# AdaLN attention and gated MLP in one kernel: output sums carried in PSUM, gates that read one factor from PSUM

## The chip, the cores and the metric

The kernel runs on one core of a Trainium2 chip. The metric is the time of one execution in device microseconds. The program is traced in the order in which it is written: each engine (PE for matmuls, DVE for vector operations, ACT for activations and copies, POOL, SP for DMA issues) works through its own queue in that order, and semaphores hold an instruction until its inputs are there and its output's old readers are done.

## The reference

One transformer block over 2048 tokens of width 576. Six modulation rows come from a small vector `c`. The first half is attention of 32 query heads of 128 over the last 512 keys of 16 cached key and value heads; the second half is an MLP of inner width 4608, gated by a rectifier.

```python
mod = (_silu(c) @ w_mod).reshape(c.shape[0], 6, 1, -1)      # sa, ca, ga, sb, cb, gb
h = _layernorm(x) * (1 + ca) + sa
x = x + ga * attention(h)         # softmax(q k^T / sqrt(128)) v, then @ wo, K and V: last 512 rows
h = _layernorm(x) * (1 + cb) + sb
gate, up = h @ W_gate, h @ W_up
x = x + gb * ((gate * (gate > 0) * up) @ W_down)
```

## The kernel before

Every large matmul is done in a split form: an operand is cut into a rounded part (`hi`) and the rest (`lo`), and three products make one. ACT makes `hi` by a copy, POOL makes `lo` by a subtraction.

**State.** `acc[0..15]` are sixteen tiles of 128 tokens x 576 in SBUF. They hold x, collect the attention's output and then the MLP's, and are stored at the end.

**Attention.** There are NU = 128 units: 16 key heads, 4 blocks of 512 tokens, 2 query heads each. The main loop (L1176 to L1225) writes out the order of one unit u by hand, with places `run(u, 0)` to `run(u, 9)` at which a table of further steps (weight loads and cuts, layer norms, modulation sums) is worked in. For unit u, PE does the scores (`s_half`, L407 to L409), the projection of the next unit's queries (`qproj`, L360), one small matmul `qm` (`spread`, L433), a first output piece, the two halves of the product with v for unit u-1 (`pv_half`, L507 to L509), and a second output piece.

DVE takes the scores' block maxima (L412), reduces them to 16 a partition (`max_pre`, L419), multiplies them by a mask of four columns (L420) and reduces the last unit's sums of exponentials (`sum_pre`, L426). `qm` spreads the masked maxima and the sums over the partitions; the tile of `qm` is a PSUM bank of the pool `psM`, which has two, shared with the projection and the product with v. Then DVE finds the maximum (L448) and the sum's inverse (L438), subtracts the maximum (L480), and ACT takes the exponential (L482) and makes its `hi` (L469). POOL sums the exponentials (L495, L498) and makes `lo` (L489).

**Output pieces.** `wo_piece` multiplies the outputs of two heads by their rows of wo for one tile of 128 tokens: 12 matmuls of 288 columns (L536) into the two banks of `psW`. That pool has one buffer, which some layer norm transposes and modulation rows use too. `down_piece` returns a function that adds the banks to `acc` on DVE (L542); the loop puts it in `pend` and calls it by `flush()` a few steps later. A piece can start only when the piece before it has been read out.

**MLP.** 36 rounds m, each with seven products P1 to P7 (a scheme in which seven products of sums of blocks do the work of eight), in the order P1, P6, P2, P7, P5, P4, P3. A product makes gate and up for 512 tokens in the two halves of a PSUM pair (`prod`, L834). P2 goes on in P1's pair and P3 in P5's. `evac` reads the pair out: running sums `q` and `r` are kept in SBUF, and four of the products end in a gate, max(gate, 0) times up, whose result `h_out` cuts into `hhi` on ACT (L849) and `hlo` on POOL (L850). Between the halves of a product stand the output pieces of the round before (`md_piece`, the same L536 and L542, `psW`). In the first 18 rounds the weights are also combined (`w_prep`: L647, L651, L652, L657 on DVE), cut (L627 on ACT, L628 and L629 on POOL) and stored for the second 18, and the rows of W_down are gated (L216) and cut (L175, L176). In rounds 2 to 15 layer norms (`ln_half`) and sums for the later tokens (`h_later`, L752, L764, L767) are worked in.

Of the kernel before, what the change touches and what calls it, by code (L numbers as in the profile page):

```python
# [32 lines left out]
def kernel(  # L33
# [119 lines left out]
    def gate_row(j):  # L153
        r = cp.tile([P, D], F32, tag="mrow", name=f"mrow{j}")
        mod_row(j, r, 0.0)
        return r
# [88 lines left out]
        else:  # L245
            nc.sync.dma_start(dst[:96], hb[qb, 4][j].rearrange("r p n -> (r p) n"))

    pend = []
    ready = {}
    adds = [0] * (S // P)  # L250

    def flush():
        while pend:
            pend.pop()()

    class LayerNorm:
        def __init__(self, qb, key, where):
# [157 lines left out]

    def max_pre(u):
        t5[u] = sp.tile([P, 5, 16], F32, tag="t5", name=f"t5_{u}", bufs=1)
        t = t5[u][:, 4, :]
        nc.vector.tensor_reduce(t, t4.pop(u).rearrange("p k b -> p b k"), axis=AX.X, op=ALU.max)  # L419
        nc.vector.tensor_tensor(t5[u][:, 0:4, :], mask[:, :, None].to_broadcast([P, 4, 16]),  # L420
                                t[:, None, :].to_broadcast([P, 4, 16]), op=ALU.mult)
# [7 lines left out]

    def spread(u):  # L430
        a, b = (0 if u < NU else 4), (5 if u else 4)
        bps[u] = psM.tile([P, 512], F32, tag="mm", name=f"qm{u}")
        nc.tensor.matmul(bps[u][:, a * 16:b * 16], quad,  # L433
                         t5.pop(u)[:, a:b, :].rearrange("p a b -> p (a b)"), start=True, stop=True)

# [89 lines left out]
    def down_piece(his, los, ws, i, qt, nm, mid=None, pool=None):  # L525
        sl = slice(qt * P, (qt + 1) * P)
        pool = pool or (psW, "w")
        ps = pool[0].tile([P, 2, 512], F32, tag=pool[1], name=nm)
        for half in range(2):
            if half and mid:  # L530
                mid()
            cs = slice(half * H2, (half + 1) * H2)
            n = 0
            for hi, lo, w in zip(his, los, ws):
                for a, b in ((hi, 0), (hi, 1), (lo, 0)):
                    nc.tensor.matmul(ps[:, half, :H2], a[:, sl], w[:, b, cs],  # L536
                                     start=(n == 0), stop=(n == 5))
                    n += 1
        av = acc[i].rearrange("p (h n) -> p h n", h=2)

        def add():
            nc.vector.tensor_tensor(av, ps[:, :, :H2], av, op=ALU.add)  # L542
            adds[i] += 1

        return add

    def wo_piece(u1, qt, mid=None):
        g, qb, h = unit(u1)
        return down_piece([ohi[u1 - 1], ohi[u1]], [olo[u1 - 1], olo[u1]], [wos[h - 1], wos[h]],
                          4 * qb + qt, qt, f"wo{u1}_{qt}", mid)  # L550

# [287 lines left out]
    def h_out(m, f, k, r):  # L839
        pool, tag = HI[f, k]  # L840
        hi = hhi[m, f, k] = pool.tile([P, 512], F32R, tag=tag, name=f"hhi{m}_{f}{k}")
        if k == 0:
            pool, tag, w = op, "olo", 512
        elif f == 1:
            pool, tag, w = qp, ("qlo", "qhi")[m % 2], 512
        else:
            pool, tag, w = xp, "xm", 640
        lo = hlo[m, f, k] = pool.tile([P, w], F32R, tag=tag, name=f"hlo{m}_{f}{k}")[:, :512]
        nc.scalar.copy(hi, r)  # L849
        nc.gpsimd.tensor_sub(lo, r, hi.bitcast(F32))  # L850

    def gated(m, f, k, c):
        nc.vector.scalar_tensor_tensor(c[:, 0, :], c[:, 0, :], 0.0, c[:, 1, :], op0=ALU.max, op1=ALU.mult)
        h_out(m, f, k, c[:, 0, :])

    npair, px = [0], {}

# [8 lines left out]
    def evac(m, s):  # L866
        ps = pair[m, s]
        if s == "P1":
            t = tmp["q"] = pp.tile([P, 2, 512], F32, tag="hi", name=f"q{m}")
            nc.scalar.copy(t, ps)  # L870
        elif s == "P2":
            r = xp.tile([P, 640], F32, tag="xm", name=f"r{m}")[:, :512]
            nc.scalar.activation(r, ps[:, 0, :], AF.Relu, bias=0.0, scale=1.0)
            nc.vector.tensor_tensor(r, ps[:, 1, :], r, op=ALU.mult)
            h_out(m, 0, 0, r)
        elif s == "P6":
            nc.vector.tensor_tensor(tmp["q"], ps, tmp["q"], op=ALU.add)
        elif s == "P7":
            t = tmp["r"] = pp.tile([P, 2, 512], F32, tag="lo", name=f"r{m}", bufs=2)
            nc.vector.tensor_tensor(t, ps, tmp["q"], op=ALU.add)  # L880
        elif s == "P5":
            t = pp.tile([P, 2, 512], F32, tag="lo", name=f"c22_{m}", bufs=2)
            nc.vector.tensor_tensor(t, ps, tmp["r"], op=ALU.add)
            gated(m, 1, 1, t)
        elif s == "P4":
            nc.vector.tensor_tensor(tmp["r"], ps, tmp["r"], op=ALU.add)
            gated(m, 1, 0, tmp["r"])
        else:
            nc.vector.tensor_tensor(tmp["q"], ps, tmp["q"], op=ALU.add)
            gated(m, 0, 1, tmp["q"])  # L890

    def wd_prep(m, f):
        tag = "wB" if f else "wC"
# [37 lines left out]
    def step(name, t, fn, *args):  # L931
        sched.append((t + PLAN.get(name, 0), len(sched), fn, args))
# [14 lines left out]
    def setd(d, k, fn):  # L947
        def go():
            d[k] = fn()
        return go  # L950
# [6 lines left out]
    def norm_steps(nm, qb, key, w2, w3, t_st, t_rs, t_nm, t_tr, t_af, how):  # L957
        ln = LayerNorm(qb, key, xms[:2] + where[w2] + where[w3])
        how = CFG.get(nm, how)
        for i in range(4):  # L960
            step(f"{nm}.st{i}", t_st[i], ln.stats, i)
        step(f"{nm}.rs", t_rs, ln.rstd)
        for i in range(4):
            step(f"{nm}.nm{i}", t_nm[i], ln.norm, i)
        for k, ds in enumerate(((0, 1), (2, 3), (4,))):
            pool = pools[how[k][0]]
            tag = {"s": "s", "w": "w", "m": "mm"}[how[k][0]]
            step(f"{nm}.tr{k}", t_tr[k], ln.trans, ds, pool, tag)
            step(f"{nm}.af{k}", t_af[k], ln.affine, ds, *((pp, "p") if qb < 2 and key == "a" else (bp, "bc")),
                 how[k][1:])  # L970

# [38 lines left out]
    step("v0.c", 1, pv0[1])  # L1010
    for t in range(5):
        step(f"m2.{t}", (4, 4, 14, 14, 16)[t], lambda t=t: mod_step(2, t, big[2, t]))
    step("ga", 19, setd(mods, "ga", lambda: gate_row(2)))
    norm_steps("a2", 2, "a", "wC", "raw", (8, 9, 14, 14), 16, (19,) * 4, (29, 26, 29),
               (29, 26, 29), (("w", "aav", "vvv"), ("w", "vvv", "vvv"), ("m", "aav")))
# [159 lines left out]
    run(-1, 9)  # L1175
    for u in range(NU):  # L1176
        u0, q0 = (u - 4, 3) if u % 2 else (u - 3, 1)
        u1, q1 = (u - 2, 0) if u % 2 else (u - 3, 2)
        run(u, 0)
# [12 lines left out]
        spread(u)  # L1192
        max_bc(u)
        if u + 1 < NU:
            q_hi(u + 1)
        run(u, 3)
        if 0 < u0 < NU - 8:
            pend.append(wo_piece(u0, q0))
        run(u, 4)
        if u:  # L1200
            pv_half(u - 1, 0)
        exp_half(u, 0)
        ksum_op(u, 0)
# [11 lines left out]
        if 0 < u1 and (q1 == 0 or u1 < NU - 8):  # L1215
            pend.append(wo_piece(u1, q1))
# [65 lines left out]
```

## Time and profile before

| | |
|---|---|
| median of 3 runs | 3110.5 us (3109.76 to 3110.93) |
| the profiled execution | 3113.83 us |
| its span, first to last instruction | 3112.0 us |
| mean granted PE clock | 0.977 |
| attention, about | 0 to 1700 us |
| MLP, about | 1700 to 3112 us |

The page has one profiled execution; its numbers are compared with that execution's own time. A group's line names the kernel line, the engine, the operation, the tiles and shapes, the count, then the busy time, the mean of one, and the idle time of the engine before the group. A line of the list of waits names who waited for whom, the total in us, the count and the longest. A line of the timeline gives the start and duration in us, and in brackets how long the engine stood before it and for whom.

### The profile page before, as it was taken

The numbers are of one execution on the slowest core, as the hardware profiler recorded it, in microseconds if no ns is written. First come the engines' busy times: TensorE is split into PE (matmuls) and PEld (weight loads), VectorE is DVE, ScalarE is ACT, GpSimd is POOL, SyncE is SP. The second block draws the span as 40 slices with busy tenths as digits, with TensorE's granted clock in tenths as the row PEclk, the third lists the DMA queues.
The fourth block names the chain that finished last, engine by engine and source line by source line (L and its number), as shares of the span: only waits on it lengthen the run. The fifth ranks groups of instructions, "written<-read, shape, count | busy, mean of one in ns | idle before, by whom it ended". The sixth has DMA issues, their size and how long they took to land. (4 is left out here: it accounts for less than half of the span.)

```text
span 3112.0 us, 40062 instructions
## 1 busy us (share of the span) xinstructions
PE 2945.5 (95%) x15414; PEld 2533.0 (81%) x15414; DVE 2225.0 (71%) x2904; ACT 1082.2 (35%) x1399; POOL 1981.7 (64%) x1386
## 2 busy tenths in 40 slices
PE   6899999999999999999987699999999999999999
PEld 5688888888888888888876588887787888888888
DVE  7888888888898888888875666666766544444444
ACT  5444444444444444444443233333222211111110
POOL 5788999888888898888975555556656311111111
PEclk9999999999999999999998799999999999999999
DMA  4101111211111100000002356557777954444443
GB/s 144 38 24 54 62 65 62 68 54 55 46 45 48 34 25 26 16 16 20 24 30 95 119 201 213 210 209 260 255 256 248 329 175 173 157 162 162 170 169 114
DMA packets 143647, 360.24 MB, mean 116 GB/s; under 512 B 12768, under 2 KB 52448, under 8 KB 143456
## 3 DMA queue, kind: packets, MB, share of 16 engines
q1 hardware_dynamic: 115312, 245.15, 24.6%
q10 hardware_dynamic: 28144, 112.54, 9.2%
q8 instruction: 121, 1.98, 0.3%
q14 instruction: 70, 0.57, 0.1%
HBM read 234.62 MB, written 151.32 MB: 124 GB/s over the span
## 5 line engine op out<-in xcount | busy, mean ns | idle before, releaser
L489 POOL TENSOR_TENSOR lo<-p,hi 128x1024 fp32r<-128x1024 f32 x256 | 607.7, 2395 | 0.0
L536 PE MATMUL md<-wogb,hhi 128*128 128x288 f32 x2304 | 482.8, 302 | 50.8 <-DVE acc L542 31.3
L834 PE MATMUL gu<-hop_T,wop 128*128 128x512 f32 (+1 forms) x2016 | 505.6, 396 | 16.5 <-ACT hop_T L684 11.7
L542 DVE TENSOR_TENSOR acc<-md,acc 128x576 f32<-128x576 f32 x288 | 217.3, 755 | 413.0 <-PE md L536 412.8
L536 PEld LDWEIGHTS md<-wogb,hhi 128*128 128x128 f32 x2304 | 391.9, 193 | 86.8 <-DVE acc L542 44.7
L834 PEld LDWEIGHTS gu<-hop_T,wop 128*128 128x128 f32 (+1 forms) x2016 | 372.4, 190 | 88.3 <-ACT hop_T L684 12.2
L536 PE MATMUL wo<-woga,ohi 128*128 128x288 f32 x2048 | 427.3, 301 | 11.0 <-DVE acc L542 9.7
L360 PE MATMUL qps<-hTa,wA 128*128 128x512 f32 x1792 | 430.5, 391 | 1.9 <-DVE hTa L344 1.1
L498 POOL TENSOR_TENSOR ks<-ks,p 128x512 f32<-128x512 f32 x256 | 345.8, 1351 | 95.1 <-ACT p L482 81.7
L360 PEld LDWEIGHTS qps<-hTa,wA 128*128 128x128 f32 x1792 | 338.4, 189 | 73.8 <-POOL hTa L348 1.8
L834 PE MATMUL gu<-hop_B,wop 128*128 128x512 f32 (+1 forms) x1512 | 388.4, 400 | 6.8 <-DVE hop_B L688 3.6
L412 DVE TRANSPOSE_TENSOR_REDUCE t<-s 128x32 f32<-128x1024 f32 x256 | 318.8, 1247 | 77.2 <-PE s L409 64.5
L536 PEld LDWEIGHTS wo<-woga,ohi 128*128 128x128 f32 x2048 | 334.0, 189 | 25.7 <-DVE acc L542 14.5
L850 POOL TENSOR_TENSOR hlo<-r,hhi 128x512 fp32r<-128x512 f32 x72 | 93.8, 1303 | 401.2 <-ACT hhi L849 334.8
L536 PE MATMUL md<-wogb,hlo 128*128 128x288 f32 x1152 | 346.0, 300 | 1.0 <-POOL hlo L850 1.0
L834 PEld LDWEIGHTS gu<-hop_B,wop 128*128 128x128 f32 (+1 forms) x1512 | 286.0, 194 | 65.6 <-DVE hop_B L688 4.0
L482 ACT ACTIVATE p<-p 128x1024 f32<-128x1024 f32 x242 | 256.0, 1058 | 137.8 <-DVE p L480 108.6
L536 PE MATMUL wo<-woga,olo 128*128 128x288 f32 x1024 | 303.0, 296 | 0.0
L480 DVE TENSOR_TENSOR p<-s,mb 128x1024 f32<-128x1024 f32 x242 | 294.9, 1219 | 3.8
L469 ACT CAST hi<-p 128x1024 fp32r<-128x1024 f32 x256 | 269.6, 1053 | 7.9
L536 PEld LDWEIGHTS md<-wogb,hlo 128*128 128x128 f32 x1152 | 222.0, 193 | 1.2 <-POOL hlo L850 1.2
L542 DVE TENSOR_TENSOR acc<-wo,acc 128x576 f32<-128x576 f32 x256 | 192.4, 751 | 39.9 <-PE wo L536 26.4
(176 smaller groups left out, 5043.5 us busy)
## 6 DMA issues: line engine op xcount, KB each, us to landing
wk_P<-wop ACTq DMA_DIRECT2D x126, 640.0 KB
wop<-wk_P SPq DMA_DIRECT2D x126, 640.0 KB
wr<-wlay SPq DMA_DIRECT2D x72, 384.0 KB
dk<-wogb ACTq DMA_DIRECT2D x36, 576.0 KB
wogb<-dk SPq DMA_DIRECT2D x36, 576.0 KB
rogb<-wd SPq DMA_DIRECT2D x36, 288.0 KB
rwA<-wq SPq DMA_DIRECT2D x32, 320.0 KB
wlay<-wg SPq DMA_DIRECT2D x36, 256.0 KB
```

Of the source, the lines that this page charges most:

```text
L360: return [lambda i=i, a=a, b=b: nc.tensor.matmul(ps, a, b, start=(i == 0), stop=(i == n - 1)) for i, (a, b) in enumerate(ops)]
L412: nc.vector.tensor_reduce(t4[u][:, 2 * h:2 * h + 2, :].rearrange("p k b -> p (k b)"), t.rearrange("p k (b j) -> p (k b) j", j=32), axis=AX ...
L469: nc.scalar.copy(hi_[u, h], pt[u, h])
L480: nc.vector.tensor_tensor(p, t, bc[u][:, None, :].to_broadcast([P, 2, 512]), op=ALU.subtract)
L482: nc.scalar.activation(p, p, AF.Exp, bias=0.0, scale=1.0)
L489: nc.gpsimd.tensor_sub(lo_[u, h], pt[u, h], hi_[u, h].bitcast(F32))
L498: nc.gpsimd.tensor_tensor(ks_[u], ks_[u], p[:, j, :], op=ALU.add)
L536: nc.tensor.matmul(ps[:, half, :H2], a[:, sl], w[:, b, cs], start=(n == 0), stop=(n == 5))
L542: nc.vector.tensor_tensor(av, ps[:, :, :H2], av, op=ALU.add)
L834: nc.tensor.matmul(ps, a, c, start=s not in ("P2", "P3") and i == 0, stop=i == len(ops) - 1, skip_group_check=True)
L850: nc.gpsimd.tensor_sub(lo, r, hi.bitcast(F32))
```

## The change

Three edits.

First, output pieces that follow another piece in `psW` with no other user between (`seeded`) no longer start their own sums. ACT copies the `acc` tile of the next piece into the banks (`put_seed`), the piece's matmuls add to it, and ACT copies the banks back to `acc`. The function that does both is put in a list of its own, `pend_act`, which is worked off ahead of `exp_half(u, 0)` for the first piece of a unit and behind `hi_half(u, 1)` for the second. Pieces that follow another user of `psW` are done as before.

Second, the gates. `gated` reads gate and up from the PSUM pair: it adds the running sum to the gate half into SBUF, adds it to the up half in place in PSUM, and takes max(gate, 0) times up with up in PSUM. P2's rectifier goes from ACT to DVE. Since P3 goes on in P5's pair, whose up half now holds a sum, P7's up half is copied by ACT into `q` and subtracted.

Third, `max_pre` writes the reduced maxima into columns 128 to 143 of the bank of `qm`, and the mask multiplies them from there; so the bank is taken in `max_pre` and not in `spread`.

```diff
+    def flush(q=None):
+        q = pend if q is None else q
+        while q:
+            q.pop()()
...
     def max_pre(u):
         t5[u] = sp.tile([P, 5, 16], F32, tag="t5", name=f"t5_{u}", bufs=1)
-        t = t5[u][:, 4, :]
+        bps[u] = psM.tile([P, 512], F32, tag="mm", name=f"qm{u}")
+        t = bps[u][:, 128:144]
         nc.vector.tensor_reduce(t, t4.pop(u).rearrange("p k b -> p b k"), axis=AX.X, op=ALU.max)
...
     def spread(u):
         a, b = (0 if u < NU else 4), (5 if u else 4)
-        bps[u] = psM.tile([P, 512], F32, tag="mm", name=f"qm{u}")
+        if u == NU:
+            bps[u] = psM.tile([P, 512], F32, tag="mm", name=f"qm{u}")
...
                     nc.tensor.matmul(ps[:, half, :H2], a[:, sl], w[:, b, cs],
-                                     start=(n == 0), stop=(n == 5))
+                                     start=(n == 0 and seed is None), stop=(n == 5),
+                                     skip_group_check=seed is not None)
...
         def add():
+            adds[i] += 1
+            if seed is not None:
+                nc.scalar.copy(av, ps[:, :, :H2])
+                return
             nc.vector.tensor_tensor(av, ps[:, :, :H2], av, op=ALU.add)
-            adds[i] += 1
...
+    w_use, pieces, seeds = set(), [], {}
+
+    def seeded(n):
+        return 0 < n < len(pieces) and not any(pieces[n - 1][0] < t <= pieces[n][0] for t in w_use)
+
+    def put_seed(n):
+        if seeded(n):
+            u1, qt = pieces[n][1:]
+            g, qb, h = unit(u1)
+            s = seeds[n] = psW.tile([P, 2, 512], F32, tag="w", name=f"wo{u1}_{qt}")
+            nc.scalar.copy(s[:, :, :H2], acc[4 * qb + qt].rearrange("p (h n) -> p h n", h=2))
+
+    def piece(n):
+        add = wo_piece(*pieces[n][1:], seed=seeds.get(n))
+
+        def end():
+            add()
+            put_seed(n + 1)
+
+        (pend_act if n in seeds else pend).append(end)
+        return n in seeds
...
-    def gated(m, f, k, c):
-        nc.vector.scalar_tensor_tensor(c[:, 0, :], c[:, 0, :], 0.0, c[:, 1, :], op0=ALU.max, op1=ALU.mult)
-        h_out(m, f, k, c[:, 0, :])
+    def gated(m, f, k, ps, r, a, op1=ALU.add):
+
+        if a is None:
+            nc.vector.tensor_scalar(r, ps[:, 0, :], 0.0, None, op0=ALU.max)
+        else:
+            nc.vector.tensor_tensor(r, ps[:, 0, :], a[:, 0, :], op=ALU.add)
+            nc.vector.tensor_tensor(ps[:, 1, :], ps[:, 1, :], a[:, 1, :], op=op1)
+        nc.vector.scalar_tensor_tensor(r, r, 0.0, ps[:, 1, :], op0=ALU.max, op1=ALU.mult)
+        h_out(m, f, k, r)
...
         elif s == "P2":
-            r = xp.tile([P, 640], F32, tag="xm", name=f"r{m}")[:, :512]
-            nc.scalar.activation(r, ps[:, 0, :], AF.Relu, bias=0.0, scale=1.0)
-            nc.vector.tensor_tensor(r, ps[:, 1, :], r, op=ALU.mult)
-            h_out(m, 0, 0, r)
+            gated(m, 0, 0, ps, xp.tile([P, 640], F32, tag="xm", name=f"r{m}")[:, :512], None)
...
         elif s == "P7":
             t = tmp["r"] = pp.tile([P, 2, 512], F32, tag="lo", name=f"r{m}", bufs=2)
             nc.vector.tensor_tensor(t, ps, tmp["q"], op=ALU.add)
+            nc.scalar.copy(tmp["q"][:, 1, :], ps[:, 1, :])
         elif s == "P5":
             t = pp.tile([P, 2, 512], F32, tag="lo", name=f"c22_{m}", bufs=2)
-            nc.vector.tensor_tensor(t, ps, tmp["r"], op=ALU.add)
-            gated(m, 1, 1, t)
+            gated(m, 1, 1, ps, t[:, 0, :], tmp["r"])
         elif s == "P4":
-            nc.vector.tensor_tensor(tmp["r"], ps, tmp["r"], op=ALU.add)
-            gated(m, 1, 0, tmp["r"])
+            gated(m, 1, 0, ps, tmp["r"][:, 0, :], tmp["r"])
         else:
-            nc.vector.tensor_tensor(tmp["q"], ps, tmp["q"], op=ALU.add)
-            gated(m, 0, 1, tmp["q"])
+
+            gated(m, 0, 1, ps, tmp["q"][:, 0, :], tmp["q"], ALU.subtract)
...
         run(u, 3)
-        if 0 < u0 < NU - 8:
-            pend.append(wo_piece(u0, q0))
+        if 10 * u + 3 in at:
+            piece(at[10 * u + 3])
         run(u, 4)
         if u:
             pv_half(u - 1, 0)
+        flush(pend_act)
         exp_half(u, 0)
...
         run(u, 8)
         hi_half(u, 1)
+        flush(pend_act)
         lo_half(u, 0)
```

More of the change, by code (lines that the diff above doesn't have):

```diff
@@ L246, in hb_load @@
             nc.sync.dma_start(dst[:96], hb[qb, 4][j].rearrange("r p n -> (r p) n"))
-    pend = []
+    pend, pend_act = [], []
     ready = {}
     adds = [0] * (S // P)
-    def flush():
-        while pend:
-            pend.pop()()
+    def flush(q=None):
+        q = pend if q is None else q
+        while q:
+            q.pop()()
     class LayerNorm:
@@ L523, in o_lo, with down_piece @@
         nc.gpsimd.tensor_sub(olo[u], o.pop(u), ohi[u].bitcast(F32))
-    def down_piece(his, los, ws, i, qt, nm, mid=None, pool=None):
+    def down_piece(his, los, ws, i, qt, nm, pool=None, seed=None):
         sl = slice(qt * P, (qt + 1) * P)
         pool = pool or (psW, "w")
-        ps = pool[0].tile([P, 2, 512], F32, tag=pool[1], name=nm)
+        ps = pool[0].tile([P, 2, 512], F32, tag=pool[1], name=nm) if seed is None else seed
         for half in range(2):
-            if half and mid:
-                mid()
             cs = slice(half * H2, (half + 1) * H2)
@@ L541, in add, with wo_piece @@
         def add():
+            adds[i] += 1
+            if seed is not None:
+                nc.scalar.copy(av, ps[:, :, :H2])
+                return
             nc.vector.tensor_tensor(av, ps[:, :, :H2], av, op=ALU.add)
-            adds[i] += 1
         return add
-    def wo_piece(u1, qt, mid=None):
+    def wo_piece(u1, qt, seed=None):
         g, qb, h = unit(u1)
         return down_piece([ohi[u1 - 1], ohi[u1]], [olo[u1 - 1], olo[u1]], [wos[h - 1], wos[h]],
-                          4 * qb + qt, qt, f"wo{u1}_{qt}", mid)
+                          4 * qb + qt, qt, f"wo{u1}_{qt}", seed=seed)
+    w_use, pieces, seeds = set(), [], {}
[14 more added lines that the diff above has]
+        return n in seeds
     NFP = NFT // 2
@@ L968, in norm_steps @@
             step(f"{nm}.tr{k}", t_tr[k], ln.trans, ds, pool, tag)
+            if tag == "w":
+                w_use.add(t_tr[k])
             step(f"{nm}.af{k}", t_af[k], ln.affine, ds, *((pp, "p") if qb < 2 and key == "a" else (bp, "bc")),
@@ L1012 @@
         step(f"m2.{t}", (4, 4, 14, 14, 16)[t], lambda t=t: mod_step(2, t, big[2, t]))
+    w_use.update((19, e - 41, e - 21))
     step("ga", 19, setd(mods, "ga", lambda: gate_row(2)))
@@ L1173, in run @@
             fn(*args)
-    run(-1, 9)
     for u in range(NU):
@@ L1178 @@
         u1, q1 = (u - 2, 0) if u % 2 else (u - 3, 2)
+        if 0 < u0 < NU - 8:
+            pieces.append((10 * u + 3, u0, q0))
+        if 0 < u1 and (q1 == 0 or u1 < NU - 8):
+            pieces.append((10 * u + 6, u1, q1))
+    at = {t: n for n, (t, _, _) in enumerate(pieces)}
+    run(-1, 9)
+    for u in range(NU):
         run(u, 0)
@@ L1214 @@
             pv_half(u - 1, 1)
-        if 0 < u1 and (q1 == 0 or u1 < NU - 8):
-            pend.append(wo_piece(u1, q1))
+        if 10 * u + 6 in at:
+            piece(at[10 * u + 6])
         run(u, 7)
```

## The prediction

> **What bounds the kernel now.** I read the page's busy times first, then busy time by stretch, then the starts of one matmul that every attention unit has once, and only then the waits.
>
> ```profile
> span 3112.0 us, 40062 instructions
> PE 2945.5 (95%) x15414; PEld 2533.0 (81%) x15414; DVE 2225.0 (71%) x2904; ACT 1082.2 (35%) x1399; POOL 1981.7 (64%) x1386
> ...
> 160.00:1580.00 1420.00, 1407.68 (x7370) 1205.27 (x7369) 1254.12 (x1771) 650.21 (x774) 1265.01 (x775) 1.00 0.13 41
> 1580.00:1790.00 210.00, 150.47 (x670) 122.14 (x669) 133.39 (x172) 72.61 (x105) 112.91 (x87) 0.84 0.26 90
> 1790.00:2440.00 650.00, 604.41 (x3171) 522.22 (x3170) 420.53 (x416) 202.34 (x293) 390.81 (x358) 0.96 0.67 233
> 2440.00:3112.00 672.00, 664.71 (x3673) 588.46 (x3671) 285.82 (x326) 77.21 (x114) 103.83 (x82) 1.00 0.51 175
> ```
>
> The columns after each stretch are its length, then PE, PEld, DVE, ACT and POOL busy, then the granted clock. PE is the bound everywhere, and the change leaves the list of matmuls as it is. So the change can win only time in which PE stands: 12 us by this view in the attention, 60 in the passage to the MLP, 46 in the MLP's first half, 7 in the second half. But a busy PE hides short stalls, since a matmul's end is modelled. The unit's own beat shows them: the start of the `qm` matmul, one pair per unit.
>
> ```profile
> 143.60 0.45 PE L433 MATMUL qm<-t,quad 128*128 128x80 f32 x2
> ...
> 1001.90 0.45 PE L433 MATMUL qm<-t,quad 128*128 128x80 f32 x2
> ...
> 1014.28 0.45 PE L433 MATMUL qm<-t,quad 128*128 128x80 f32 x2
> ...
> 1063.18 0.34 PE L433 MATMUL qm<-t,quad 128*128 128x80 f32 x2
> ...
> 1076.76 0.45 PE L433 MATMUL qm<-t,quad 128*128 128x80 f32 x2 [0.54 <-DVE t L426]
> ...
> 1432.58 0.34 PE L433 MATMUL qm<-t,quad 128*128 128x80 f32 x2
> ...
> 1480.84 0.34 PE L433 MATMUL qm<-t,quad 128*128 128x80 f32 x2
> ...
> 1578.34 0.34 PE L433 MATMUL qm<-t,quad 128*128 128x80 f32 x2
> ```
>
> From 1432.58 to 1480.84 lie four units in which `qm` is not held: 12.06 us each. The unit 1001.90 to 1014.28 took 12.38, that from 1063.18 to 1076.76 took 13.58. From 143.60 to 1578.34 are 116 units; at 12.06 they would take 1399, and they took 1434.7. So 36 us are lost in the attention's steady part, three times what the busy column shows. What holds `qm`:
>
> ```profile
> PEld qm L433 <- DVE t L426: 45.7, 66, 3.8
> ...
> 1010.93 4.75 POOL L489 TENSOR_TENSOR lo<-p,hi 128x1024 fp32r<-128x1024 f32 x2
> ...
> 1012.67 0.74 DVE L420 TENSOR_TENSOR t<-mask,t 128x64 f32<-128x64 f32 x1
> 1013.51 0.71 DVE L426 TRANSPOSE_TENSOR_REDUCE t<-ks 128x16 f32<-128x512 f32 x1
> ...
> 722.91 1.41 POOL L176 TENSOR_TENSOR woga<-roga,woga 128x576 fp32r<-128x576 f32 x1
> ...
> 725.94 0.23 DVE L420 TENSOR_TENSOR t<-mask,t 128x64 f32<-128x64 f32 x1
> ...
> L420 DVE TENSOR_TENSOR t<-mask,t x128: 224/564/2169, 42.3 to 1686.3; 128x64 f32<-128x64 f32 x128
> ```
>
> L420 multiplies 64 elements a partition. With POOL idle (at 725.94, POOL's last row ended at 724.32) it takes 0.23; in the unit of 1014.28 it takes 0.74 and ends at 1013.41, just behind the first of POOL's two L489 (half of 4.75 after 1010.93 is 1013.3). It waits for POOL while both read SBUF. Behind it stands L426, and `qm` waits for L426.
>
> **The change part by part.** (1) L420 gets its maximum from PSUM, so one of its inputs leaves SBUF. Does that free it of POOL? The MLP's rows answer:
>
> ```profile
> L853 DVE SCALAR_TENSOR_TENSOR r<-r x36: 691/694/3518, 1761.9 to 3092.0; 128x512 f32<-128x512 f32 x36
> ...
> L880 DVE TENSOR_TENSOR r<-gu,q x36: 1206/1225/1226, 1749.1 to 3081.1; 128x1024 f32<-128x1024 f32 x36
> ```
>
> With both inputs in SBUF (L853) the longest is five times the median; with one in PSUM (L880) the longest equals the median. So I take 0.23 for L420 (bounds: 0.22, its minimum, and 0.56, its median now). L426 ends 0.5 us earlier; it was late by about 0.33 (12.38 less 12.06), so nearly all these waits go. 66 waits are listed in the whole run; some 60 lie in the steady part, at 0.36 (0.33, and more in a few long ones): -22. The wait that comes next is that for DVE's two L412 before it, which the 0.23 leaves 0.2 or more ahead of PE. The bank of `qm` is taken earlier, in front of the next projection; two banks are free then, nothing waits.
>
> (2) A piece's sum leaves DVE for two ScalarE copies: out to `acc`, then the next piece's seed.
>
> ```profile
> L542 DVE TENSOR_TENSOR acc<-wo,acc 128x576 f32<-128x576 f32 x256 | 192.4, 751 | 39.9 <-PE wo L536 26.4
> ...
> PE wo L536 <- DVE acc L542: 9.7, 13, 3.0
> ...
> 1003.48 0.63 ACT L519 CAST ohi<-rb 128x512 fp32r<-128x512 f32 x1 [7.01 <-PE wo L536]
> ...
> 1004.01 0.59 ACT L387 ACTIVATE qhi<-qps 128x512 fp32r<-128x512 f32 x1
> ...
> 1004.50 0.66 ACT L175 CAST woga<-roga 128x576 fp32r<-128x576 f32 x1
> ...
> 1006.56 0.42 PE L536 MATMUL wo<-woga,ohi 128*128 128x288 f32 x2
> ...
> L870 ACT COPY q<-gu 128x1024 f32<-128x1024 f32 x36 | 36.6, 1016 | 103.0 <-PE gu L834 47.7 <-POOL wop L629 38.9 <-PE pv L508 6.2
> ```
>
> DVE loses some 230 adds of 0.75, 1.5 us a unit, off the bound. ACT gains two copies a piece. No row shows ACT writing PSUM; the nearest are L175, 0.66 for 576 elements within SBUF, and L870, 1.02 for 1024 out of PSUM. I take 0.65, so 1.3 a pair (bounds 1.2 and 2.04). ACT goes from 650 of 1420 us to about 950: room enough. The point is place: the first pair stands ahead of the exponential of its unit, and piece two now waits for it. In the tight unit (every second one, where `ohi` waits for the first piece) `qhi` ends at 1004.60 and piece two starts at 1006.56: 1.96 for a pair of 1.3. Where the cast of `woga` stands there too (one unit in eight, the one shown), 1.96 for 1.96, and PE would wait 0.3 or so: 15 units, +4. The exponentials come 0.6 to 0.9 later; behind them wait POOL's L495, L498 and L489. POOL is busy 1265 of 1420, so it takes this up in its waits for `p`; `lo` is then ready about 1 us before PE reads it, where it was 2. I cost that at nothing; if POOL fell back one more cast (1.4 us) in one unit of eight, it would be +5. The waits for DVE's add in the attention's long units (13.58) and a shorter DVE queue before the column sums of the modulation give back the rest:
>
> ```profile
> 718.41 0.58 PE L164 MATMUL mps<-ones,macc 128*128 128x1 f32 x2 [2.00 <-DVE macc L161]
> ...
> 718.00:724.00 6.00, 5.59 (x14) 4.53 (x15) 1.77 (x3) 0.00 (x0) 6.00 (x4) 0.50 0.00 0
> ...
> 1589.94 2.17 DVE L420 TENSOR_TENSOR t<-mask,t 128x64 f32<-128x64 f32 x1
> ...
> 1593.08 0.42 PE L433 MATMUL qm<-t,quad 128*128 128x80 f32 x2 [1.58 <-DVE t L426]
> ```
>
> In front of L161 stood an add of 0.75, so of the 2.00 some 0.7 go, and with ten long units at 0.4 I take -4.5. The last units before the MLP hold the worst L420 (2.17); its wait of 1.58 goes, others there shrink by 0.5 each: -3. Units before 143 us: -1.
>
> The row of 718 to 724 has clock 0.50 after a wait of 2.00; if the shorter wait keeps the clock, up to 3 us more are won there, which I keep for the range. [...]
>
> (3) Gating. P5, P4 and P3 have now a 1024 add out of PSUM (1.23) and L853; after, two 512 adds and L853 with its second factor in PSUM. A 512 of L853 without POOL is 0.69, so three are 2.07 against 1.92: +0.15 each. P2 loses ACT's step and gains one of 0.69 on DVE, P7 gains a 0.6 copy on ACT. P3's matmuls go on in P5's bank and now wait for P5's L853, not its first add; between lies the whole product of P4. P7's copy waits for P7's add on DVE, and behind it in ACT's queue stand the next stores' issues and the cast of the weights for three products later, behind that cast POOL's L628 and L629: all with products to spare. In the MLP's second half DVE is busy 286 of 672: hidden behind the next product, 0; without that cover it would be 0.45 + 0.69 in each of 36 rounds, 41 us. In the first half DVE is late:
>
> ```profile
> PE md L536 <- DVE acc L542: 31.3, 20, 5.0
> DVE r L874 <- ACT r L873: 68.3, 36, 4.2
> ...
> 2250.50 3.52 DVE L853 SCALAR_TENSOR_TENSOR r<-r 128x512 f32<-128x512 f32 x1
> ...
> 2248.86 1.28 POOL L850 TENSOR_TENSOR hlo<-c,hhi 128x512 fp32r<-128x512 f32 x1 [2.29 <-ACT hhi L849]
> ...
> 2252.04 1.42 POOL L176 TENSOR_TENSOR wogb<-rogb,wogb 128x576 fp32r<-128x576 f32 x1
> 2254.75 1.26 POOL L850 TENSOR_TENSOR hlo<-r,hhi 128x512 fp32r<-128x512 f32 x1 [1.29 <-ACT hhi L849]
> ```
>
> PE waits 31 us for DVE's adds. Here L853 took 3.52, until POOL's run from 2248.86 to 2253.46 ended. Freed of that, it would take 0.69. But right behind it DVE has the weights' differences (L651, L652), both inputs in SBUF, and they would meet the same run of POOL: the wait moves on more than it goes. What stays won is one L853, 0.7, in each of 18 rounds, less 0.3 of longer adds: -7. Bounds: all of the 31 us, and some clock with them, -40; and +16 (below).
>
> [...]
>
> **Sum:** -22 + 4 - 4.5 - 3 - 1 + 0 - 7 = -33.5. The profiled execution took 3113.8 with its span of 3112.0, so 3080; the median of the runs, 3110.5, is 3.3 lower: 3077.
>
> **Rivals.** The first half clears too: L651 and L652 slip in before POOL's run, and the clock stays up; 25 us more, 3052. For it: L874's waits for ACT vanish from DVE's queue. Against: POOL's run is there whatever DVE does.
>
> The moved wait grows: a quicker gate makes `hhi` quicker, so POOL goes on into `hlo` of r (1.3, the row at 2254.75) before L651 gets its turn. 18 rounds at 1.3 in place of -0.4 are +23: the stage loses 16 and not wins 7, 3100. For it: POOL's gap of 1.29 at 2254.75 is there only because DVE was late.
>
> Seeds come late (slower): PE waits at piece two, in every second unit, from a pair longer than 1.96 on. It turns the sign where 58 such units lose 33.5 us, 0.58 each, a pair of 2.5; at 2.7 it is 43 us, 3120. Against: it is above the upper bound of 2.04.
>
> It doesn't do what it says: an input in PSUM does not spare L420. Then the 22 stay, and L853 stays as it is: about -4.5 -1 +4, 3109. Against: L880's flat durations.
>
> **How the numbers follow.** Forecast 0.64, clears too 0.13, moved wait 0.12, seeds late 0.06, no effect 0.05. The range takes in the first three, the -40 of the first half too (3044), and a pair at its bound of 2.04 (0.1 in 58 units, 0.7 in 15, less the 4: +12): 3044 to 3103. A measurement can tell about 0.2%, 6 us, from no change. Faster: 0.64 + 0.13 + most of 0.12 = 0.87; same: the rest of it and the 0.05, 0.07; slower: 0.06.
>
> **What would show it.** Right: L420 with a longest near its shortest, the list of waits without `qm` for L426, 12.1 us from `qm` to `qm`, L853 flat at 0.69, and longer L651 and L652. Wrong: PE waiting for ScalarE at `wo`, PE waiting for `lo` at L509, ACT copies of 576 above 0.98, or more waits at `md` than 31 us.

## The result, and the profile after

The changed kernel takes 3063.3 us (median of 4 runs, 3058.6 to 3067.9); the kernel before, run beside it on the same chip, 3110.7. The ratio is 0.9845, with a 95% interval of 0.9827 to 0.9863: 47 us faster, where 33.5 were forecast. The profiled execution took 3058.6, the shortest of the four, and the profiled one before 3113.8, so the two traces differ by 55 us and not by 47; the rest of this section explains the 55. Stage by stage it is read from these two traces, and the table below gives the other runs beside them.

The page of the changed kernel, span and busy times:

```profile
span 3056.8 us, 40707 instructions
PE 2914.2 (95%) x15414; PEld 2533.1 (83%) x15414; DVE 2027.2 (66%) x2810; ACT 1360.2 (44%) x1875; POOL 1988.1 (65%) x1386
```

The matmuls are the same 15414, and PE's busy time is nonetheless 31 us less. Since both kernels run the same matmuls in the same order, a stage's gain can be read as the difference between the starts of the same matmul. Busy time in the stretch from the first steady `qm` to the last, before and after (columns as in the prediction: length, PE, PEld, DVE, ACT, POOL, clock):

```profile
143.60:1578.34 1434.74, 1422.42 (x7445) 1218.03 (x7445) 1267.07 (x1787) 656.93 (x781) 1277.76 (x783) 1.00 0.13 41
```
```profile
144.20:1551.71 1407.51, 1406.00 (x7445) 1226.47 (x7444) 1075.37 (x1555) 931.20 (x1245) 1276.47 (x783) 1.00 0.13 42
```

The same 7445 matmuls take 27.2 us less: 12.13 a unit against 12.37. DVE gave up 192 us, ACT took on 274. And the stretch of the MLP's first half whose 3171 matmuls took 650.00 us before:

```profile
1761.09:2386.87 625.78, 591.18 (x3171) 514.93 (x3170) 400.85 (x481) 199.06 (x292) 397.82 (x358) 0.98 0.68 242
```

24.2 us less. Only 11.0 of that is time in which PE stood (650.00 less 604.41 is 45.6 before, 625.78 less 591.18 is 34.6 now). The other 13.2 is PE itself being quicker over the same matmuls, and the mean clock of the stretch rose from 0.96 to 0.98.

Single lines of the changed kernel (shortest, median and longest in ns, then first and last start). L422 is the old L420, L889 the old L853; L546 and L570 are the copy out and the seed:

```profile
L422 DVE TENSOR_TENSOR t<-mask,qm x128: 220/221/223, 41.7 to 1654.6; 128x64 f32<-128x64 f32 x128
...
L546 ACT COPY acc<-wo x238: 624/635/647, 111.0 to 1573.1; 128x576 f32<-128x576 f32 x119
...
L570 ACT COPY wo<-acc x238: 635/644/647, 107.1 to 1568.5; 128x576 f32<-128x576 f32 x119
...
L889 DVE SCALAR_TENSOR_TENSOR c<-c,gu x36: 686/686/689, 1724.4 to 3032.2; 128x512 f32<-128x512 f32 x36
```

L422's longest is 3 ns above its shortest; before, it reached 2169. L889 is as flat, where L853 reached 3518. Both now take one operand from PSUM.

A unit with a cast of `woga` in front of the pair, where a wait of PE was forecast:

```profile
985.79 0.59 ACT L388 ACTIVATE qhi<-qps 128x512 fp32r<-128x512 f32 x1
986.28 0.67 ACT L175 CAST woga<-roga 128x576 fp32r<-128x576 f32 x1
986.85 0.65 ACT L546 COPY acc<-wo 128x576 f32<-128x576 f32 x1
987.52 0.64 ACT L570 COPY wo<-acc 128x576 f32<-128x576 f32 x1
...
988.35 0.43 PE L537 MATMUL wo<-woga,ohi 128*128 128x288 f32 x2
```

The seed ends at 988.16 and piece two starts at 988.35, with no wait. In the stretch from 160 to 1580 the lists of waits of PE and of its weight loads have no `qm` in them; outside it, at the two ends of the attention, 5 waits of the weight load for the old L426 are left, 10.1 us of the 45.7. The head of PE's list, and the head of the same list from 1761 to 2387 (total us, count, longest):

```profile
PE wo L537 <- ACT acc L546: 2.8, 1, 2.8
...
PE md L537 <- ACT lflh L849: 16.2, 8, 2.8
PE md L537 <- DVE acc L548: 16.0, 10, 4.0
```

The first line is one of the prediction's signs of being wrong, PE waiting for ScalarE at `wo`, but it is a single wait: at 1573.83, where the copy out of the last seeded piece stands in ACT's queue behind the exponentials of its unit. PE's waits for DVE's adds at `md` fell from 31.3 to 16.0; those for ACT's `lflh` (L849, the old L819: the layer norm's scale and shift), 11.3 before, grew to 16.2.

By stage, in us against the kernel before, from the starts of the same matmuls (boundaries at 144, 1578, 1705, 1790 and 2440 us of the kernel before; one profiled execution each; what lies ahead of 144 came out 0.5 to 5.4 us longer in every run and is left out):

| | steady attention | last units and passage | round 0 of the MLP | MLP, first half | rest |
|---|---|---|---|---|---|
| forecast | -22.5 | -3 | 0 | -7 | 0 |
| the change | -27.1 | -5.6 | +3.3 | -24.2 | -2.1 |
| the change, profiled again | -28.5 | -5.5 | +3.3 | -20.0 | -2.2 |
| maximum alone | -21.5 | -3.7 | +0.4 | -2.0 | -1.4 |
| seeds alone | +73.7 | +3.2 | 0.0 | -2.4 | -0.7 |
| gates alone | -1.3 | +2.0 | +4.0 | -19.4 | +0.5 |
| without seeds | -21.5 | -5.7 | +3.3 | -18.1 | -0.8 |
| without gates | -28.8 | -5.5 | -0.3 | -2.7 | -1.4 |
| P2's rectifier alone | 0.0 | 0.0 | -0.6 | -8.8 | +0.9 |
| second factor in PSUM alone | -1.6 | +2.1 | +4.5 | -14.9 | -1.1 |
| P7's copy later | -27.2 | -5.6 | -0.8 | -24.6 | -1.2 |
| P7's copy later, profiled again | -27.0 | -5.6 | -0.9 | -25.5 | -0.7 |
| seed twice | -12.8 | -3.6 | +3.2 | -20.2 | -0.3 |
| seed three times | +43.0 | -3.8 | +3.3 | -20.2 | -1.0 |

### The profile page after: what moved, and what is told of

It is laid out like the page before. It is cut to its first block, busy times and chain, and to the rows that moved or that the text cites. A ratio compares the mean times of both kernels' runs of the same rounds, so it can differ in the third digit from the quotient of the medians.

```text
span 3056.8 us, 40707 instructions
## 1 busy us (share of the span) xinstructions
PE 2914.2 (95%) x15414; PEld 2533.1 (83%) x15414; DVE 2027.2 (66%) x2810; ACT 1360.2 (44%) x1875; POOL 1988.1 (65%) x1386
## 5 line engine op out<-in xcount | busy, mean ns | idle before, releaser
L864 PE MATMUL gu<-hop_T,wop 128*128 128x512 f32 (+1 forms) x2016 | 507.1, 396 | 18.3 <-ACT hop_T L714 11.1
L537 PE MATMUL md<-wogb,hhi 128*128 128x288 f32 x2304 | 477.0, 299 | 40.3 <-ACT lflh L849 16.2
L864 PEld LDWEIGHTS gu<-hop_T,wop 128*128 128x128 f32 (+1 forms) x2016 | 372.7, 190 | 91.1 <-ACT hop_T L714 12.0
L537 PE MATMUL wo<-woga,ohi 128*128 128x288 f32 x2048 | 428.6, 302 | 13.2 <-DVE acc L548 8.5
L864 PE MATMUL gu<-hop_B,wop 128*128 128x512 f32 (+1 forms) x1512 | 382.9, 396 | 4.7 <-DVE hop_B L718 3.6
L537 PEld LDWEIGHTS wo<-woga,ohi 128*128 128x128 f32 x2048 | 333.6, 190 | 26.7 <-DVE acc L548 10.1
L880 POOL TENSOR_TENSOR hlo<-r,hhi 128x512 fp32r<-128x512 f32 x72 | 100.8, 1400 | 384.8 <-issue 240.8
L864 PEld LDWEIGHTS gu<-hop_B,wop 128*128 128x128 f32 (+1 forms) x1512 | 281.8, 191 | 62.3 <-DVE hop_B L718 4.0
L483 DVE TENSOR_TENSOR p<-s,mb 128x1024 f32<-128x1024 f32 x242 | 285.0, 1219 | 3.8
L879 ACT CAST hhi<-r 128x512 fp32r<-128x512 f32 x72 | 44.7, 621 | 416.8 <-DVE r L889 334.9
```

The source lines that it names most:

```text
L483: nc.vector.tensor_tensor(p, t, bc[u][:, None, :].to_broadcast([P, 2, 512]), op=ALU.subtract)
L537: nc.tensor.matmul(ps[:, half, :H2], a[:, sl], w[:, b, cs], start=(n == 0 and seed is None), stop=(n == 5), skip_group_check=seed is not None)
L864: nc.tensor.matmul(ps, a, c, start=s not in ("P2", "P3") and i == 0, stop=i == len(ops) - 1, skip_group_check=True)
```

## The experiments

Diffs are against the changed kernel where nothing else is said. The times are medians of 2 to 10 runs, each ratio against runs of the kernel before on the same chip.

**The maximum alone.** The third edit, with the output pieces and the gates as before.

```diff
-        return 0 < n < len(pieces) and not any(pieces[n - 1][0] < t <= pieces[n][0] for t in w_use)
+        return False and not any(pieces[n - 1][0] < t <= pieces[n][0] for t in w_use)
```
Beside this line, `gated` and the branches P2, P7, P5, P4 and P3 of `evac` are those of the kernel before.

> Only the maximum moves to PSUM; sums and gates as before. Theory A (L420's wait for POOL is what holds qm): L420 flat at 0.22, the 116 steady units take 1407 to 1412 us in place of 1434.7, so 3110.7 - 24 - 4 for the units at both ends = 3083 (3078 to 3089), MLP as before. Theory B (DVE's load holds qm, the adds above all): L420's share is 0.4 us of DVE time a unit, a fifth of what leaves DVE in all, so 5 us of the 27: 3105.

Measured 3087.3 us, ratio 0.9921 (0.9905 to 0.9938). The steady attention gains 21.5 us, and the multiplication is as flat as in the whole change:

```profile
L422 DVE TENSOR_TENSOR t<-mask,qm x128: 220/221/223, 43.8 to 1663.1; 128x64 f32<-128x64 f32 x128
```

So this edit by itself frees the multiplication from POOL. What is left of the loss is six units of 12.9 us, one of 12.6 and the two with a modulation column (17.0 and 13.6), against 12.08 for nearly all others.

**The seeds alone.** The first edit; the maximum stays in SBUF and the gates are as before.

```diff
-        bps[u] = psM.tile([P, 512], F32, tag="mm", name=f"qm{u}")
-        t = bps[u][:, 128:144]
+        t = t5[u][:, 4, :]
```

> Only the output sums move to ScalarE; the maximum stays in SBUF and the gates are as before. Theory A: the exponentials come 0.6 to 0.9 later, so POOL's first L489 of a unit ends later, L420 is held longer and qm with it: the steady units get slower, by 0.1 to 0.4 each, 3120 to 3155. Theory B: 1.5 us of DVE time a unit go, so most of the 27 us go: 3085 to 3095. A third way is no effect: 3108 to 3113.

Measured 3191.5 us, ratio 1.0256 (1.0241 to 1.0271): 79 us slower, more than the expected 3120 to 3155, and all of it in the attention. The multiplication (L421 in this kernel), then one unit in the timeline, and last a line of the waits of the whole run:

```profile
L421 DVE TENSOR_TENSOR t<-mask,t x128: 224/1414/2384, 42.0 to 1766.7; 128x64 f32<-128x64 f32 x128
```
```profile
1015.66 0.63 ACT L545 COPY acc<-wo 128x576 f32<-128x576 f32 x1
1016.32 0.64 ACT L569 COPY wo<-acc 128x576 f32<-128x576 f32 x1
1017.44 4.71 POOL L491 TENSOR_TENSOR lo<-p,hi 128x1024 fp32r<-128x1024 f32 x2
...
1018.24 1.68 DVE L421 TENSOR_TENSOR t<-mask,t 128x64 f32<-128x64 f32 x1
1020.02 0.71 DVE L427 TRANSPOSE_TENSOR_REDUCE t<-ks 128x16 f32<-128x512 f32 x1
...
1020.79 0.45 PE L435 MATMUL qm<-t,quad 128*128 128x80 f32 x2 [1.00 <-DVE t L427]
...
PEld qm L435 <- DVE t L427: 140.1, 121, 3.8
```

The first of POOL's two `lo` runs from 1017.44 to about 1019.8. L421 starts inside it and ends at 1019.92, just behind it. In the prediction's unit before, the same multiplication started 1.74 us into POOL's pair (1012.67 after 1010.93); here it starts 0.80 into it, so it waits longer, and its median goes from 0.56 to 1.41. The other units say the same: over 115 steady units the median start into POOL's run falls from 2.07 to 1.06 us, and the multiplication ends 0.08 us behind an instruction of POOL's pair in 114 of them before and in all of them here. In the changed kernel the median start is 1.07, as early as here, and the multiplication takes 0.22. The pair of copies stands ahead of the exponential, the exponential ahead of POOL, and so POOL's run moved towards the multiplication. In the list of waits of the whole run the weight load of `qm` waits 140.1 us for L427, where the kernel before has 45.7: 94 us more, enough for the 79 lost.

**The gates alone.** The second edit, without the other two.

> Only the gates read their factor from PSUM; attention as before. If the first half's 24 us are the gates' own: attention 0, first half -20 to -27, 4 us lost in the first round, 3090 (3086 to 3096). If the forecast's step holds (the wait moves to L651 and L652) and the rest of the 24 came from elsewhere (the phase in which the MLP starts): 3100 to 3108.

Measured 3097.4 us, ratio 0.995 (0.9935 to 0.9965), just above the expected range. The MLP's first half gains 19.4 us, well over the forecast's 7, and round 0 loses 4.0. In the first half PE stands 7.0 us less (38.6 after 45.6, table below), which is the forecast's number; the other 12.4 are PE's own busy time.

**P7's copy later.** ACT copies P7's up half one product later, as part of P5's evacuation.

```diff
         elif s == "P7":
...
-            nc.scalar.copy(tmp["q"][:, 1, :], ps[:, 1, :])
+            tmp["p7"] = ps
         elif s == "P5":
+            nc.scalar.copy(tmp["q"][:, 1, :], tmp["p7"][:, 1, :])
```

> The changed kernel with ScalarE's copy of P7's up half issued in P5's place, one product later. If that copy, waiting for DVE, held the casts of hop_T behind it in round 0, the 4 to 5 us lost there come back and nothing else moves: 3058 to 3061 against 3063. If the loss there was only the phase of DVE and POOL: 3063, within 2.

Measured 3059.5 us, ratio 0.9828 (0.9814 to 0.9843). Round 0 gains 0.8 where the change loses 3.3. The timeline of round 0 in the changed kernel, and the same place with the copy later:

```profile
1715.78 1.22 DVE L913 TENSOR_TENSOR r<-gu,q 128x1024 f32<-128x1024 f32 x1
...
1717.09 0.59 ACT L914 COPY q<-gu 128x512 f32<-128x512 f32 x1 [18.87 <-DVE r L913]
1718.30 1.66 ACT L714 CAST hop_T<-hr 128x512 fp32r<-128x512 f32 x3
1718.95 3.25 DVE L718 TENSOR_TENSOR hop_T<-hr,hop_T 128x512 fp32r<-128x512 f32 x1 [1.96 <-ACT hop_T L714]
...
1722.26 4.62 PE L864 MATMUL gu<-hop_T,wop 128*128 128x512 f32 x12 [2.55 <-DVE hop_T L718]
```
```profile
1715.10 6.60 PE L864 MATMUL gu<-hop_T,wop 128*128 128x512 f32 x28
...
1717.10 0.68 DVE L718 TENSOR_TENSOR hop_T<-hr,hop_T 128x512 fp32r<-128x512 f32 x1
1717.27 0.59 ACT L916 COPY q<-gu 128x512 f32<-128x512 f32 x1 [13.07 <-DVE r L913]
```

In the changed kernel ACT stands at the copy for DVE's sum of P7, and behind it in ACT's queue are the casts of the next products' operand `hop_T` (L714), which DVE and then PE wait for. With the copy behind those casts, PE runs through 28 matmuls. The same run repeated with the changed kernel beside it:

> The changed kernel with P7's copy on ACT issued one product later, against the changed kernel on the same chip. Theory A: the round-0 loss of 5 us is gone and stays gone: 4 to 6 us below the changed kernel's time. Theory B: the lower time of the first look was scatter: within 2 us of it.

> The changed kernel once more, beside the others on one chip: 3063 (3058 to 3068).

Measured 3058.1 (ratio 0.9822, 0.9808 to 0.9837) and 3066.2 us (0.9851, 0.9834 to 0.9867): 8 us apart on one chip, a little more than was expected. This version beats both kernels. In round 0 it regains 4. The rest is not accounted for. PE's waits at `md` for ACT's `lflh` are back from eight to four (16.2 us to 11.2), but those for DVE's adds grew in their place, and PE stands 35.4 and 33.0 us in the first half of this version's two traces, against 34.6 and 35.8 in those of the change.

**P2's rectifier alone, and the second factor alone.** To split the gates' gain: first P2 on DVE as in the change with the other gates as before, then the other gates as in the change with P2's rectifier on ACT. The diff is the first one's, against the kernel before.

```diff
-            nc.scalar.activation(r, ps[:, 0, :], AF.Relu, bias=0.0, scale=1.0)
-            nc.vector.tensor_tensor(r, ps[:, 1, :], r, op=ALU.mult)
+            nc.vector.tensor_scalar(r, ps[:, 0, :], 0.0, None, op0=ALU.max)
+            nc.vector.scalar_tensor_tensor(r, r, 0.0, ps[:, 1, :], op0=ALU.max, op1=ALU.mult)
```

> Of the gates only P2's: its rectifier goes from ScalarE to DVE and up is read from PSUM; P5, P4 and P3 as before, no copy of P7's up half. Theory C (what the gates won is DVE's queue no longer standing for ScalarE, 68 us of waits of L874 before): 12 us or more of the 19 that the first half won, 3095 to 3100. Theory D (it is the factor left in PSUM, L853 no longer held by POOL): 0 to 4 us, 3108 to 3113.

> Of the gates only P5's, P4's and P3's factor in PSUM, with the copy of P7's up half; P2 as before. Theory D: L853 flat at 0.69 and its 46 us over that gone, the first half wins 15 to 20, the first round loses 4 to 5: 3096 to 3101. Theory C: 0 to 5 won and the same loss: 3110 to 3117. The forecast's step (the wait moves on): L651 and L652 grow by more than 20 us in all.

Measured 3106.2 us, ratio 0.9982 (0.9972 to 0.9992), and 3103.8, ratio 0.9969 (0.9959 to 0.998). Both fall between the two theories: neither piece is the gates' gain by itself. By medians they give 6 and 9, together the 15 of the gates alone; the loss in round 0 belongs to the factor, with its copy of P7 (+4.5 against -0.6). Over the same 3171 matmuls, with the count of stretches of 3.41 us at half clock (why 3.41 is in the last section):

| | length, us | PE busy | PE standing | stretches at half clock |
|---|---|---|---|---|
| before | 650.0 | 604.4 | 45.6 | 14 |
| without gates | 647.3 | 601.7 | 45.6 | 13 |
| P2's rectifier alone | 641.2 | 598.1 | 43.1 | 10 |
| second factor alone | 635.1 | 594.6 | 40.5 | 11 |
| gates alone | 630.6 | 592.1 | 38.6 | 9 |
| the change, profiled again | 630.0 | 594.2 | 35.8 | 9 |
| the change | 625.8 | 591.2 | 34.6 | 7 |

I estimate, from the recorded clock of 0.50, that each such stretch costs half its length of PE's work, 1.7 us (the pace of the matmuls, in the last section, gives 1.6): seven fewer are 12 of the 13.2 us by which PE's busy time fell in the change. The count does not cover every row as well: in the second factor alone it gives 5 of 9.8, in the gates alone 8.5 of 12.4, and what the rest is stays open. The two executions of the changed kernel differ by two, 3.4 by the count of the 4.2 us between them.

**The seed twice and three times.** `put_seed` issues the same copy into the banks once or twice more; the last one stands, so the values are the same and only the pair is longer.

```diff
+            nc.scalar.copy(s[:, :, :H2], acc[4 * qb + qt].rearrange("p (h n) -> p h n", h=2))
             nc.scalar.copy(s[:, :, :H2], acc[4 * qb + qt].rearrange("p (h n) -> p h n", h=2))
```

> The changed kernel with each seed copied twice, so 1.9 us of ScalarE between a piece and the next. Seeds-late theory: only the tight units with a cast of woga (one in eight, 0.19 to spare) wait, 0.45 each and some 0.2 for the restart: 15 x 0.65, 3070 to 3075. If ScalarE's room (44% busy) covers it: 3063, within 4.

> The changed kernel with each seed copied three times, 2.55 us between pieces. Seeds-late theory: every second unit waits at piece two, 0.4 in 45 of them and 1.1 in 15, and the exponentials are 1.3 later, so POOL's sums may come behind L428's turn: 3095 to 3120. If ScalarE's room covers it: 3063, within 4.

Measured 3085.4 us, ratio 0.9911 (0.9891 to 0.9931), and 3142.4, ratio 1.0094 (1.0074 to 1.0114): 22 and 79 us over the changed kernel's first median, both more than expected. The waits of the weight loads in the stretch from 160 to 1580, seed twice and then three times (total us, count, longest):

```profile
PEld wo L537 <- ACT wo L571: 21.8, 58, 0.8
```
```profile
PEld wo L537 <- ACT wo L572: 86.3, 111, 1.5
```

With a pair of 1.92 (0.635 and twice 0.644) every tight unit, 58 of them, is held, though piece two had 1.96 by the prediction. A tight unit of the changed kernel without a cast shows why:

```profile
1011.12 0.64 ACT L570 COPY wo<-acc 128x576 f32<-128x576 f32 x1
...
1012.29 0.41 PEld L537 LDWEIGHTS wo<-woga,ohi 128*128 128x128 f32 x2
...
1012.51 0.42 PE L537 MATMUL wo<-woga,ohi 128*128 128x288 f32 x2
```

The seed is needed by the weight load at 1012.29, 0.22 ahead of the matmul, and ended 0.53 before it. A copy more (0.67 from start to start) is 0.14 late there, and in the 15 cast units, which had nothing left to the load, 0.67: 43 by 0.14 and 15 by 0.67 are 16 us, beside the 14.3 and 15.7 by which this kernel's steady part is slower than the two executions of the change. With 2.57 piece two is held in nearly every unit and not only in the tight ones: 111 waits, one a unit, of about 0.5 us where there was none and 0.9 to 1.5 in the tight units. Between the two the sign turns: -27 against the kernel before at 1.92, +30 at 2.57, so near 2.2 by a straight line.

**Without seeds, and without gates.** The change less one of its edits, to see what each is worth in the others' company.

> The whole change without its seeds: every output piece starts its own sum and DVE adds it to acc, as before; the maximum in PSUM and the gates stay. Theory A: with the maximum in PSUM the seeds pay, by what the lag of the changed kernel (-32.2 us at 1705 us) has more than that of the maximum alone (-23.7): 8.5 us, so 3072 (3069 to 3076). Theory B: the seeds give nothing even there, and the 8.5 us are scatter of two executions: 3063 (3060 to 3066).

> The maximum in PSUM and the seeds, with the gates as before. Theory A: the stages add up, so the attention's -33.9 us at 1740 us stays, and the MLP gives what it gave with the maximum alone, -3: 3074 (3070 to 3078). Theory B: part of the gain of the MLP's first half came from ACT's and DVE's queues being emptier at its entry and not from the gates: below 3068.

Measured 3073.5 us, ratio 0.9875 (0.986 to 0.9889), and 3083.5, ratio 0.9901 (0.9884 to 0.9918). Seeds that cost 79 us alone give 7 once the maximum is in PSUM (3073.5 less 3066.2 in the same batch); theory A holds. Without the gates the median came out above theory A's 3070 to 3078 (before was 3114.2 in this batch, 3.7 above its first median); its profiled execution, the fastest at 3077.2, has the attention's gain whole and 2.7 us in the first half, so theory B, a gain of the first half that doesn't need the gates, falls. The other three runs are 6 to 9 us above that execution, and no trace shows where they lose it.

## Why the prediction was right, and where it was wrong

**The multiplication, -22: right.** 21.5 measured with this edit alone, and by the mechanism named: 220 to 223 ns whatever POOL does, no `qm` among PE's waits from 160 to 1580 in the change.

**The pair's place, +4: wrong in size and sign.** The price of 0.65 for each copy was right (635 and 644 ns). The row "1.96 for 1.96, PE would wait 0.3 or so: 15 units" failed: the three instructions of the cast unit ran from 986.28 to 988.16, 1.88 instead of 1.96, and they began 0.1 us before the recorded end of `qhi`; piece two came 0.19 after the seed. Together with the -4.5 for long units and the modulation column the seeds were to give 0.5; they gave 5.6 in the steady part (27.1 less 21.5), since six long units went from 12.9 to 12.08 whole. The wait at the column shrank from 2.00 to 1.39 us with the seeds, near the forecast's 0.7. That it saved the clock, for which 3 us were kept in the range, is not shown: behind this wait the kernel before has two stretches of 3.41 us at half clock, the change one, the maximum alone also one, though its wait is still 1.97, and the second trace of the change none.

**POOL's casts one pair later, "I cost that at nothing": right only in company.** Seeds alone showed the cover of this zero: it is the maximum in PSUM. The prediction asked whether `lo` would be late for PE. What happened is that POOL's run met DVE's multiplication earlier, and the kernel lost 79 us, with PE waiting at `qm`. The text did not see that one edit paid for the other's side effect.

**The units before 143 us, -1:** not seen; the change is 0.5 us later there. **The last units, -3:** 5.6, of which the maximum alone gives 3.7 and, without seeds, maximum and gates 5.7. **The second half, 0:** right; from 2480 us on, the difference of the two traces stays at 55.2.

**P7's copy, "all with products to spare": wrong in round 0.** There the casts of the next products' operands (L714), which the prediction did not list behind the copy, have no product to spare: 4 us, shown by moving the copy.

**The MLP's first half, -7: the mis-sized term.** Of the 21.7 us by which the profiled execution beats its forecast of 3080.3, 17.2 lie here. Two things were in it. First, "the wait moves on more than it goes". L853's groups before, and the sums and differences of the weights, before and then after (busy us, mean ns; L677, L681, L682 and L687 are the old L647, L651, L652 and L657):

```profile
L853 DVE SCALAR_TENSOR_TENSOR r<-r 128x512 f32<-128x512 f32 x36 | 44.9, 1247 | 1.2
...
L853 DVE SCALAR_TENSOR_TENSOR q<-q 128x512 f32<-128x512 f32 x36 | 40.9, 1136 | 1.2
...
L853 DVE SCALAR_TENSOR_TENSOR c<-c 128x512 f32<-128x512 f32 x36 | 35.5, 986 | 1.2
...
L652 DVE TENSOR_TENSOR wr<-ws,wr 128x768 f32<-128x768 f32 x18 | 30.8, 1710 | 4.0 <-POOL wop L629 1.9
...
L651 DVE TENSOR_TENSOR wr<-wr,wr 128x768 f32<-128x768 f32 x18 | 21.3, 1184 | 0.0
...
L657 DVE TENSOR_TENSOR wr<-wr,wr 128x768 f32<-128x768 f32 x18 | 19.3, 1073 | 8.3 <-POOL wop L629 8.3
...
L647 DVE TENSOR_TENSOR ws<-wr,wr 128x768 f32<-128x768 f32 x18 | 17.1, 949 | 0.0
```
```profile
L681 DVE TENSOR_TENSOR wr<-wr,wr 128x768 f32<-128x768 f32 x18 | 33.7, 1873 | 0.0
...
L682 DVE TENSOR_TENSOR wr<-ws,wr 128x768 f32<-128x768 f32 x18 | 21.2, 1176 | 4.0 <-POOL wop L659 1.9
L687 DVE TENSOR_TENSOR wr<-wr,wr 128x768 f32<-128x768 f32 x18 | 20.6, 1144 | 11.8 <-POOL wop L659 11.7
L677 DVE TENSOR_TENSOR ws<-wr,wr 128x768 f32<-128x768 f32 x18 | 20.2, 1125 | 0.0
```

L853 took 121.3 us for 108 instructions; at 0.687 they are 74.2, so 47 us of waiting went. L651 grew by 12.4, but L652, which was to grow too, shrank by 9.6: the pair of them took up 2.8, and with L647 and L657 the four took up 7.2 (88.5 to 95.7). So most of the wait went, and did not move on. Even so PE's standing fell by only 11.0, and in the gates alone by 7.0. That the forecast's 7 is near is luck, since its reason was the wait moving on; why so few of DVE's 47 us reach PE stays open. Second, the clock: the prediction gave it no term in this stage, only a place in the range, and PE's busy time fell by 13.2 us, of which the count of half-clock stretches covers 12. The forecast of 3077 missed mainly by that.

**The rivals.** The first half did clear in part, as the first rival had it, with the clock up; 3063 lies nearer to its 3052 than to 3077, and the honest reading is that both were half right. The moved wait did not grow. (Its words put 1.3 a round in place of the -0.4; its sum, from a gain of 7 to a loss of 16, adds the 1.3.) No effect is refuted by the maximum alone. Seeds that come late are a real mechanism: a pair of 1.92 in place of 1.28 costs 22 us. By the prediction's rule the sign, with the 47 us really won, would turn at 1.96 plus 47 over 58, 2.8; it turns near 2.2, since the load is needed 0.22 ahead of the matmul, and at 2.57 piece two of nearly every unit is held, not only of every second.

## What to carry to other kernels

Ask of every zero in a sum which other edit covers it: the seeds cost 79 us or give 7, depending on one operand's memory. Where PE stands for two microseconds or so at a time, cost the clock with the wait, for here it was about half of what the stage gained (12 of 24.2 us by the count of stretches at half clock). And an instruction that waits for another engine is better issued behind those in its queue that others need sooner: here that gave 4 us.

## What the runs showed of the hardware that was not expected

**The clock changed on a grid.** In the traces of both kernels the records of the granted clock are 1.00 or 0.50 (26 of 52 records at 0.50 before, 20 of 40 after) and change only at multiples of 3.41 us from the first change. The 128x512 matmuls of a product (L834, now L864) follow each other at a median of 0.227 us at 1.00 and of 0.427 at 0.50, in both. The same wait of 2.8 us of PE for `lflh` (L849) lies twice in the changed kernel; the windows are cut on the grid, first at 1876, then at 1954 (second number PE's busy time, third from the end the clock):

```profile
1876.35:1879.76 3.41, 1.87 (x10) 1.22 (x8) 0.79 (x2) 2.55 (x5) 1.86 (x2) 1.00 0.91 310
1879.76:1883.18 3.42, 2.16 (x15) 2.08 (x16) 0.27 (x1) 1.20 (x3) 2.69 (x3) 1.00 0.74 267
1883.18:1886.59 3.41, 3.15 (x15) 2.20 (x13) 1.71 (x2) 0.81 (x2) 0.00 (x0) 1.00 1.00 345
...
1954.85:1958.26 3.41, 0.95 (x7) 0.95 (x8) 0.00 (x0) 2.40 (x6) 3.41 (x4) 1.00 0.62 225
1958.26:1961.68 3.42, 3.42 (x13) 2.94 (x13) 0.76 (x1) 0.00 (x0) 0.48 (x1) 0.51 1.02 354
```

Split over two windows, which it leaves 1.87 and 2.16 us busy, the wait is followed by a window at 1.00; with all but 0.3 us of it in one it leaves 0.95 of 3.41 busy, and the next window's clock is 0.51. Over the fourteen traces, from 1500 us on and at full clock, a window in which PE stood 1.0 to 1.7 us was followed by half clock in 4 of 210 cases, from 1.9 us on in 210 of 212, and between the two in 17 of 36. In the two traces compared above alone the counts are 0 of 26, 33 of 33 and 2 of 3. So these two equal waits differ by about 1.7 us, by the estimate above, through where they fall, and that is part of the scatter between executions of one kernel: the MLP's first half has 7 and 9 stretches at half clock in the two executions of the changed kernel.

**A later neighbour can cost more than a longer one.** In the seeds alone L427, for which PE's `qm` waits, took 0.71 us as L426 did before, and POOL's pair 4.71 in the unit shown against 4.75; DVE's multiplication, 0.224 us at its shortest, came to a median of 1.41, from 0.56, with POOL's run 1.0 us nearer to it (the median start into it 1.06 after 2.07).
